# A gated state-space and MLP kernel: the first 512 tokens laid out four to a partition

## The chip, the cores and the metric

The kernel runs on one core of a Trainium2 chip. The time is the device time of one execution in microseconds, as the median of several runs. A profile of one execution stands beside it; its span leaves out what lies around the instructions.

## The reference

The input is x, 2048 tokens of 448 features in bf16. Two branches are computed and mixed by a gate of each token:

```python
g = sigmoid((x * gate_w).sum(-1, keepdims=True))
# branch A: a diagonal state-space layer
dt = exp(log_dt); Lam_bar = exp(dt * Lam)                # Lam = Lambda_re + i Lambda_im, 448 states
B_bar = ((Lam_bar - 1) / Lam)[:, None] * (B_re + i B_im)
Bu = einsum("bld,pd->blp", x, B_bar)
h[t] = Lam_bar * h[t-1] + Bu[t]                          # over the 2048 tokens
a = 2 * einsum("blp,dp->bld", h, C_re + i C_im).real + x * Dskip
# branch B: an MLP
b = silu(x @ w1) @ w2                                    # 448 -> 1792 -> 448
out = g * a + (1 - g) * b
```

## The kernel before

The tokens are cut into four stretches of 512 (`CH`), each of four blocks of 128. All of it is written as a list of operations with reads, writes, an estimated cost and a priority. A planner (`Plan.order`) lays them in order: TensorE's operations stay in the written order, those of the other engines are taken as they come ready by the estimates. It also gives each PSUM result its bank or pair of banks. `Waits` then puts semaphores between the engines, and the order is fixed before the kernel runs.

For a stretch `tc`:

- *Load* (lines 401 and 402 for the first stretch, `load_xn` for the others): x arrives in `xnat` as [128 partitions, block, 448]. The token of partition p and block b is 128 b + p. The first stretch comes in two transfers of two blocks each, `xn00` on SP's queue and `xn01` on ScalarE's, each the first of its queue; the first columns of w1 follow behind them in the same two queues.
- *Turning* (`x0_transposes` for the first stretch, line 478; `x_transposes`, line 508): TensorE transposes the blocks, VectorE and ScalarE copy the results into `xT` (lines 486 and 488; 516 and 518), features on partitions and the stretch's 512 tokens side by side, block after block.
- *Products* (`x_products`, line 663): two tiles at a time share a pair of PSUM banks. An "F" tile is 128 of the 1792 columns of x @ w1; ScalarE evicts it with SiLU into `aT`. A "B" tile is one of the seven slots of real and imaginary parts of U, the input of the states. `evict` copies U out of PSUM: for the first stretch VectorE (line 640, three evictions of two tiles and one of one tile), for the others ScalarE (line 642).
- *Lanes* (`lanes`): VectorE rotates U by tables of sines and cosines, runs the recurrence as a scan along the 512 columns (line 736), and rotates back into `H[tc]`, seven slots of 512 columns. The scan needs the columns in time order.
- *MLP output* (`ffn2`, line 774): for each block, 14 matmuls with the block's 128 columns of `aT` as weights; ScalarE scales by 1 - g, and a DMA adds the result to `Tb` (which is `xnat`'s space and already holds g x Dskip).
- *Readout* (`readout`, line 795): for each block, seven matmuls with 128 columns of `H[tc]` as weights and the output weights `CP` as the moving side; VectorE multiplies by g and adds `Tb` (line 798) into one of five buffers `ot`, and SP stores the 128 rows (line 801).

The gate (`gates`) works on `xnat` rows, each partition by itself. TensorE's written order is: products of the first stretch (eight F tiles, the seven B tiles, six F tiles) and, with the second stretch's turning in between, the second stretch's B tiles; then the readout weights and the MLP output of the first stretch; the F tiles of the second stretch, and so on. The first stretch's readout stands behind the second stretch's MLP output.

Of the kernel before, what the change touches and what calls it, by code (L numbers as in the profile page):

```python
# [17 lines left out]
CH = 512  # L18
# [3 lines left out]
NSLOT = 7  # L22
NOT = 5
# [253 lines left out]
def bass_gated_mix__ssm_conv_s5__dense_activation_silu__prompt_kernel(nc, A_x, A_Lambda_re, A_Lambda_im, A_B_re, A_B_im, A_C_re, A_C_im,  # L277
               A_log_dt, A_Dskip, B_x, B_w1, B_w2, gate_w, out):
    with ExitStack() as ctx:
        E = ctx.enter_context  # L280
        P = Plan()

        def sb(name, shape, dtype):
            return E(nc.sbuf_tensor(name, list(shape), dtype))

        x2, out2 = A_x[0], out[0]

        xnat = sb("xnat", [128, NTB, D_MOD], BF16)
# [4 lines left out]
        CP = sb("CP", [128, NSLOT, D_MOD], BF16)  # L293
# [6 lines left out]
        H = [H2C[:, 0:3584].rearrange("p (s n) -> p s n", s=NSLOT) if k == 2 else sb(f"H{k}", [128, NSLOT, CH], BF16) for k in range(4)]  # L300
# [11 lines left out]
        ot = [sb(f"ot{k}", [128, D_MOD], BF16) for k in range(NOT)]  # L312
# [41 lines left out]
        def sem():  # L354
            _s[0] += 1
            return E(nc.semaphore(name=f"d{_s[0]}"))

        def bk(t, k=0):
            return ps[:, t.bank + k, :]

        def bk2(t):
            return ps[:, t.bank:t.bank + 2, :]
# [4 lines left out]
        def act_cost(n, aps=0):  # L367
            return 0.17 + n * 0.000833 + 0.09 * aps
# [4 lines left out]
        def ACT(fn, r, w, cost, prio, tag=""):  # L373
            return P.add("act", fn, r, w, cost, prio, tag=tag)

        def DVE(fn, r, w, cost, prio, tag=""):
            return P.add("dve", fn, r, w, cost, prio, tag=tag)
# [4 lines left out]
        def PE(fn, r, w, cost, tag=""):  # L382
            return P.add("pe", fn, r, w, cost, 0, tag=tag)
# [3 lines left out]
        def load(q, dst, src, name, nbytes, prio=None, after=()):  # L387
            nl[0] += 1
            prio = nl[0] if prio is None else prio
            P.add(q, lambda e: e.dma_start(dst, src), list(after), name.split(), 0.6 if q == "pool" else 0.5, prio, sem(), nbytes, tag="ld " + name)  # L390
# [3 lines left out]
        def load_w1(q, k, a, b):  # L394

            cols = slice(w1cuts[k], w1cuts[k + 1])
            src = B_w1[320:448, cols] if a == 3 else B_w1[128 * a:128 * b, cols].rearrange("(b p) f -> p b f", p=128)
            load(q, w1s[:, 3, cols] if a == 3 else w1s[:, a:b, cols], src, " ".join(f"w1_{k}_{i}" for i in range(a, b)),
                 256 * (b - a) * (cols.stop - cols.start))

        for h, q in enumerate(("sp", "act")):
            load(q, xnat[:, 2 * h:2 * h + 2, :], x2[256 * h:256 * h + 256, :].rearrange("(b p) d -> p b d", p=128), f"xn0{h}", 256 * 896)
        load_w1("sp", 0, 0, 2)
        load_w1("act", 0, 2, 3)
        load_w1("act", 0, 3, 4)
# [217 lines left out]
        def evict(pair, tk):  # L623

            kinds = [t[0] for t in pair]
            for k, n in ((0, 2),) if pair[0][:2] == pair[-1][:2] and len(pair) == 2 else ((0, 1), (1, 1))[:len(pair)]:
                kind, tc, a = pair[k]
                step = pair[k + 1][2] - a if n == 2 else 1
                sl = slice(a, a + step * (n - 1) + 1, step)
                names = [t[2] for t in pair[k:k + n]]  # L630
                src = (lambda: bk2(tk)) if n == 2 else (lambda k=k: bk(tk, k)[:, None, :])
                if kind == "F":
                    dst = aT[tc % 2][:, sl, :]
                    ACT(lambda e, src=src, dst=dst: e.activation(dst, src(), AF.Silu),  # L634
                        [tk, "tbl"], [f"aT{tc % 2}_{m}" for m in names], act_cost(512 * n), 2.5, "silu")
                    continue
                U, un = UG[tc % 2], f"U{tc % 2}_"
                dst = U[:, sl, :]
                if tc == 0:
                    DVE(lambda e, src=src, dst=dst: e.tensor_copy(dst, src()), [tk], [f"{un}{m}" for m in names], 0.15 + 0.53 * n, 2.6, "U")  # L640
                else:
                    ACT(lambda e, src=src, dst=dst: e.activation(dst, src(), AF.Copy), [tk], [f"{un}{m}" for m in names], act_cost(512 * n), 5, "U")  # L642
                if 3 in names:
                    load("pool", U[0:64, 7, :], U[64:128, 3, :], un + "7a", 65536, 9, [un + "3"])
                    load("pool", U[64:128, 7, :], U[0:64, 3, :], un + "7b", 65536, 9, [un + "3"])

        def x_products(tiles, fill={}, wait=()):
# [22 lines left out]
            def half(k, h):  # L670
                if h == 0 and pairs[k][0] == ("F", 0, 0):
                    def zero(pe):
                        for n in range(NFILL):
                            for b, p in enumerate((slice(64, 128), slice(0, 64))):
                                r = pe.matmul(bk(toks[k], b)[:, 0:128], ones[p, 0:128], ones[p, 0:128], start=True, stop=True)  # L675
                        return r
                    PE(zero, [], [toks[k]], NFILL * 0.11, "fill")
                    steps(k, 0, 0, 2)
                    steps(k, 0, 2, 4)
                else:  # L680
                    steps(k, h, 0, len(part[h])).own = h == 1
                if h:
                    evict(pairs[k], toks[k])
# [102 lines left out]
        def readout(tb):  # L786
            tc, o = tb // 4, (tb % 4) * 128
            t0 = tb * 128
            cuts = [(0, D_MOD)] if tb + 1 < NTB else [(0, 192), (192, 320), (320, D_MOD)]
            for n, (a, b) in enumerate(cuts):  # L790
                tk = Ps()

                def mm(pe, tk=tk, a=a, b=b):
                    for s in range(NSLOT):
                        r = pe.matmul(bk(tk)[:, 0:b - a], H[tc][:, s, o:o + 128], CP[:, s, a:b], start=(s == 0), stop=(s == NSLOT - 1))  # L795
                    return r
                PE(mm, [f"H{tc}_{s}" for s in range(7)] + [f"CP{s}" for s in range(NSLOT)], [tk], NSLOT * (0.0025 + (b - a) / 2400), f"C{tc}")
                DVE(lambda e, tk=tk, a=a, b=b: e.scalar_tensor_tensor(ot[tb % NOT][:, a:b], bk(tk)[:, 0:b - a], g[:, tb:tb + 1],  # L798
                                                                      Tb[:, tb, a:b], ALU.mult, ALU.add),
                    [tk, f"g_{tc}", f"Tb{tb}"], [f"ot{tb % NOT}{n}"] if len(cuts) > 1 else [f"ot{tb % NOT}{m}" for m in range(3)], 0.2 + (b - a) / 960, 3, "out")  # L800
                P.add("sp", lambda e, a=a, b=b: e.dma_start(out2[t0:t0 + 128, a:b], ot[tb % NOT][:, a:b]),
                      [f"ot{tb % NOT}{n}"], [], 0.3, 1, outs[tb % NOT], 128 * 2 * (b - a), tag="st")

        def readout_weights(k):
# [56 lines left out]
        def C(*tbs):  # L861
            return [lambda tb=tb: readout(tb) for tb in tbs]
# [56 lines left out]
```

## Time and profile before

| what | value |
|---|---|
| median of the runs | 141.48 us (141.35, 141.48, 143.88) |
| profiled execution | 141.25 us, span 139.5 us |
| TensorE busy | 135.9 us, 97% of the span |
| VectorE busy | 122.0 us, 87% |
| ScalarE busy | 90.3 us, 65% |
| issue of the first x loads to landing | 2.9 us (SP), 3.2 us (ScalarE), 224 KB each |
| granted TensorE clock | 0.998 of full speed |

In the profile's rows, PE is TensorE's matmuls, PEld its weight loads, DVE is VectorE, ACT ScalarE, POOL GpSimd, SP the engine that issues most transfers. A group's row has the line of the code, the engine, the operation, out<-in with shapes, the count, then busy time and mean ns of one, then the idle time of the engine before them and what ended it. A timeline row begins with start and duration in us from the span's start. Matmuls are pipelined: one of 512 columns is drawn with about 0.38 us, but they follow each other faster.

### The profile page before, as it was taken

Reading aid. Unit: us, or ns where it says so; the run is one execution under the profiler, and the core shown is the slowest. Engines: PE = TensorE matmul, PEld = TensorE weight load, DVE = VectorE, ACT = ScalarE, POOL = GpSimd, SP = SyncE. Lnnn points to the kernel's source line nnn. Section 1 sums busy time; section 2 is a strip of 40 time slices with the busy share of each in tenths; the row PEclk is TensorE's granted clock in tenths of the full one; section 3 lists DMA queues with packets and bytes.
Section 4 is the critical chain, followed back from the end, with each engine's and each line's share of the span. In section 5 each row is a group of like instructions: output and inputs, shape, how many; then the busy total and the mean of one; then the engine's idle time right before and its main releaser. Section 6 shows DMA issues by size and latency. Waiting matters only on the chain.

```text
span 139.5 us, 3000 instructions
## 1 busy us (share of the span) xinstructions
PE 135.9 (97%) x1201; PEld 67.0 (48%) x1201; DVE 122.0 (87%) x179; ACT 90.3 (65%) x157; POOL 39.2 (28%) x72
## 2 busy tenths in 40 slices
PE   7999999999999999999999999999999999999992
PEld 2445454455544544455544544444455555555561
DVE  0319999999999999999999999999999999997053
ACT  3349768999989999823694887799931268312300
POOL 7134040100248440227733001824000314022220
PEclk9999999999999999999999999999999999999999
DMA  4998999510156770104976200674202322323242
GB/s 136 337 294 243 363 320 238 177 42 0 31 79 94 129 110 1 38 15 73 157 131 155 38 5 0 95 133 79 38 4 97 66 33 36 83 83 61 40 94 71
DMA packets 17956, 14.71 MB, mean 105 GB/s; under 512 B 2835, under 2 KB 17814, under 8 KB 17942
## 3 DMA queue, kind: packets, MB, share of 16 engines
q0 software_dynamic: 6064, 5.51, 24.8%
q1 hardware_dynamic: 11318, 8.65, 20.7%
q10 hardware_dynamic: 560, 0.36, 0.8%
q8 instruction: 9, 0.15, 0.4%
q14 instruction: 5, 0.04, 0.1%
HBM read 7.17 MB, written 1.84 MB: 65 GB/s over the span
## 4 chain that ended last, share of the span: by engine, by line
PE 97%; DVE 0%; issue 0%
PE ps L663 46%; PE ps L774 31%; PE ps L795 15%; PE ps L463 2%; PE ps L508 1%; PE ps L478 1%; PE ps L814 1%; PE ps L604 1%; DVE ot L798 0%; PE ps L675 0%; PE ps L464 0%; PE ps L536 0%
## 5 line engine op out<-in xcount | busy, mean ns | idle before, releaser
L663 PE MATMUL ps<-xT,w1s 64*128 64x512 bf16 x392 | 48.5, 378 | 0.0
L774 PE MATMUL ps<-w2s,aT 128*128 128x448 bf16 x224 | 43.2, 353 | 0.0
L634 ACT ACTIVATE aT<-ps 128x1024 bf16<-128x1024 f32 (+1 forms) x30 | 28.7, 969 | 8.5 <-PE ps L663 8.4
L774 PEld LDWEIGHTS ps<-w2s,aT 128*128 128x128 bf16 x224 | 21.7, 98 | 20.4 <-ACT xnat L849 0.4
L663 PEld LDWEIGHTS ps<-xT,w1s 64*128 64x128 bf16 x392 | 19.7, 94 | 22.3 <-DVE xT L486 0.7
L663 PE MATMUL ps<-xT,BT 64*128 64x512 bf16 x196 | 25.8, 376 | 0.0
L782 POOL DMA_DIRECT2D xnat<-fe x16 | 14.1, 900 | 37.9 <-ACT fe L780 37.2
L780 ACT ACTIVATE fe<-ps,g 128x448 bf16<-128x448 f32 x16 | 10.1, 632 | 21.1 <-PE ps L774 21.0
L390 POOL DMA_DIRECT2D UG<-Gf x27 | 14.7, 549 | 20.9 <-DVE Gf L736 20.4
L736 DVE TENSOR_TENSOR_SCAN Gf<-rc,gin,H 128x512 f32<-128x512 f32 x14 | 17.2, 1268 | 0.0
L795 PE MATMUL ps<-CP,H 128*128 128x448 bf16 (+2 forms) x98 | 16.4, 326 | 0.0
L663 PEld LDWEIGHTS ps<-xT,BT 64*128 64x128 bf16 x196 | 10.8, 94 | 11.1 <-DVE Gf L562 0.2
L798 DVE SCALAR_TENSOR_TENSOR ot<-ps,g,xnat 128x448 bf16<-128x448 f32 (+2 forms) x18 | 10.8, 622 | 6.0 <-issue 4.6
L390 POOL DMA_DIRECT2D UG<-UG x8 | 4.8, 597 | 29.2 <-ACT UG L642 17.4
L704 DVE TENSOR_TENSOR H<-UG,COS 128x3584 bf16<-128x3584 bf16 (+4 forms) x10 | 12.6, 1266 | 0.0
L795 PEld LDWEIGHTS ps<-CP,H 128*128 128x128 bf16 x98 | 8.9, 98 | 7.5 <-DVE k L752 0.4
L642 ACT ACTIVATE UG<-ps 128x1024 bf16<-128x1024 f32 (+1 forms) x12 | 10.7, 923 | 1.4 <-PE ps L663 1.4
L842 ACT ACTIVATE junk<-xg 128x448 bf16<-128x448 bf16 x16 | 9.2, 574 | 2.1 <-DVE xg L704 2.0
L849 ACT ACTIVATE xnat<-xnat,g 128x448 bf16<-128x448 bf16 x16 | 9.8, 671 | 0.2
L704 DVE TENSOR_TENSOR PI<-UG,SIN 128x512 bf16<-128x512 bf16 (+2 forms) x13 | 9.1, 722 | 0.0
L704 DVE TENSOR_TENSOR PO<-UG,SIN 128x1536 bf16<-128x1536 bf16 (+1 forms) x8 | 8.7, 1087 | 0.1
L736 DVE TENSOR_TENSOR_SCAN Gf<-rc,gin,H2C 128x512 f32<-128x512 f32 x7 | 8.5, 1265 | 0.0
(102 smaller groups left out, 126.5 us busy)
## 6 DMA issues: line engine op xcount, KB each, us to landing
UG<-Gf POOLq DMA_DIRECT2D x21, 128.0 KB, 2.5
xnat<-fe POOLq DMA_DIRECT2D x16, 112.0 KB, 2.6
out_dram<-ot SPq DMA_DIRECT2D x15, 112.0 KB, 1.7
w2s<-in_B_w_dram SPq DMA_DIRECT2D x1, 1568.0 KB, 11.8
xnat<-in_A_x_dram SPq DMA_DIRECT2D x3, 448.0 KB, 6.1
w1s<-in_B_w_dram SPq DMA_DIRECT2D x1, 576.0 KB, 6.2
UG<-UG POOLq DMA_DIRECT2D x8, 64.0 KB, 2.2
H2C<-in_A_C_re_dram SPq DMA_DIRECT2D x2, 196.0 KB
```

Of the source, the lines that this page charges most:

```text
L390: P.add(q, lambda e: e.dma_start(dst, src), list(after), name.split(), 0.6 if q == "pool" else 0.5, prio, sem(), nbytes, tag="ld " + name)
L634: ACT(lambda e, src=src, dst=dst: e.activation(dst, src(), AF.Silu), [tk, "tbl"], [f"aT{tc % 2}_{m}" for m in names], act_cost(512 * n), 2 ...
L642: ACT(lambda e, src=src, dst=dst: e.activation(dst, src(), AF.Copy), [tk], [f"{un}{m}" for m in names], act_cost(512 * n), 5, "U")
L663: r = pe.matmul(bk(toks[k], b), weights(tile, p0, p0 + 64, i), xT[p0:p0 + 64, i, tc * CH:(tc + 1) * CH], start=(h == 0 and n == 0), stop=( ...
L704: DVE(lambda e: e.tensor_tensor(o, a, b, op), r, w, dve_cost(n, 2), prio, tag)
L736: DVE(lambda e, s=s, b=b, init=init: e.tensor_tensor_scan(Gf[:, s, :], rc[:, b:b + 1].to_broadcast([128, CH]), A[:, s, :], init, ALU.mult, ...
L774: r = pe.matmul(bk(tk)[:, 0:D_MOD], aT[tc % 2][:, fb, o:o + 128], w2s[:, fb, :], start=(fb == 0), stop=(fb == NFB - 1))
L780: ACT(lambda e: e.activation(f[:, :], bk(tk)[:, 0:D_MOD], AF.Copy, scale=g1[:, tb:tb + 1]), [tk, f"g1_{tc}"], [fn], act_cost(448, 1), 7, "fe")
L782: P.add("pool", lambda e: e.dma_start(Tb[:, tb, :], f[:, :], accum_op=ALU.add), [fn, f"Tb{tb}"], [f"Tb{tb}"], 0.94, 2, sem(), 115000, tag= ...
L795: r = pe.matmul(bk(tk)[:, 0:b - a], H[tc][:, s, o:o + 128], CP[:, s, a:b], start=(s == 0), stop=(s == NSLOT - 1))
L798: DVE(lambda e, tk=tk, a=a, b=b: e.scalar_tensor_tensor(ot[tb % NOT][:, a:b], bk(tk)[:, 0:b - a], g[:, tb:tb + 1], Tb[:, tb, a:b], ALU.mul ...
L849: ACT(lambda e, tb=tb: e.activation(Tb[:, tb, :], xnat[:, tb, :], AF.Copy, scale=g[:, tb:tb + 1]), [f"xd{tc}", f"g_{tc}"], [f"Tb{tb}"], ac ...
```

## The change

Only the first stretch is touched, in four places.

- *Load:* partition p takes the four neighbouring tokens 4p to 4p + 3; block b holds token 4p + b. The two transfers still bring two blocks each, so a partition's part of one transfer is two neighbouring rows of x, 1792 bytes in one piece.
- *Eviction of U* (line 640): `xT`, and with it the product in PSUM, now has its columns in the order (block, partition). The VectorE copy reads it in that order and writes column (b, t) to place 4 t + b, so U is in time order again.
- *Readout* (line 796 after): the weights of block tb are the columns tb, tb + 4, tb + 8, ... of `H[0]`.
- *Store* (lines 802 and 803 after): block tb's 128 rows go to the rows 4p + tb of the output.

What works token by token (F tiles, gate, `ffn2`, `Tb`) stays as it is, in the new order of tokens.

```diff
-            load(q, xnat[:, 2 * h:2 * h + 2, :], x2[256 * h:256 * h + 256, :].rearrange("(b p) d -> p b d", p=128), f"xn0{h}", 256 * 896)
+            load(q, xnat[:, 2 * h:2 * h + 2, :], x2[0:CH, :].rearrange("(p b) d -> p b d", b=4)[:, 2 * h:2 * h + 2, :], f"xn0{h}", 256 * 896)
...
                 if tc == 0:
-                    DVE(lambda e, src=src, dst=dst: e.tensor_copy(dst, src()), [tk], [f"{un}{m}" for m in names], 0.15 + 0.53 * n, 2.6, "U")
+                    DVE(lambda e, src=src, dst=dst: e.tensor_copy(dst.rearrange("p s (t b) -> p s b t", b=4), src().rearrange("p s (b t) -> p s b t", b=4)), [tk], [f"{un}{m}" for m in names], 0.15 + 0.53 * n, 2.6, "U")
...
-                        r = pe.matmul(bk(tk)[:, 0:b - a], H[tc][:, s, o:o + 128], CP[:, s, a:b], start=(s == 0), stop=(s == NSLOT - 1))
+                        h = H[tc][:, s, o:o + 128] if tc else H[0][:, s, tb:CH:4]
+                        r = pe.matmul(bk(tk)[:, 0:b - a], h, CP[:, s, a:b], start=(s == 0), stop=(s == NSLOT - 1))
...
-                P.add("sp", lambda e, a=a, b=b: e.dma_start(out2[t0:t0 + 128, a:b], ot[tb % NOT][:, a:b]),
+                rows = out2[t0:t0 + 128] if tc else out2[0:CH].rearrange("(p b) d -> p b d", b=4)[:, tb, :]
+                P.add("sp", lambda e, a=a, b=b, rows=rows: e.dma_start(rows[:, a:b], ot[tb % NOT][:, a:b]),
                       [f"ot{tb % NOT}{n}"], [], 0.3, 1, outs[tb % NOT], 128 * 2 * (b - a), tag="st")
```

## The prediction

> **What bounds the kernel now.** I read the busy table and the slices first, then the chain that ended last, then the groups of the touched lines by form, then the timeline and the waits of the two stretches that the change touches: the start, and the end of the first stretch's products.
>
> ```profile
> span 139.5 us, 3000 instructions
> PE 135.9 (97%) x1201; PEld 67.0 (48%) x1201; DVE 122.0 (87%) x179; ACT 90.3 (65%) x157; POOL 39.2 (28%) x72
> PE   7999999999999999999999999999999999999992
> DVE  0319999999999999999999999999999999997053
> DMA  4998999510156770104976200674202322323242
> PE 97%; DVE 0%; issue 0%
> ```
>
> TensorE is busy in every slice but the first and the last, and the chain is TensorE from 0.76 us to the last eviction. So the time moves only if TensorE starts its real work at another time, works longer, or stops in the middle. VectorE is full from slice 3 on and has room only in the last five slices. The DMA row is full from slice 1 to 6: the opening loads go as fast as the queues move bytes.
>
> The groups of the touched instructions (count | busy us, mean ns | idle before):
>
> ```profile
> L795 PE MATMUL ps<-CP,H 128*128 128x448 bf16 x28 | 5.5, 352 | 0.0
> L795 PEld LDWEIGHTS ps<-CP,H 128*128 128x128 bf16 x28 | 2.7, 98 | 2.6
> L640 DVE CAST UG<-ps 128x1024 bf16<-128x1024 f32 x3 | 3.6, 1216 | 0.0
> L640 DVE CAST UG<-ps 128x512 bf16<-128x512 f32 x1 | 0.7, 682 | 0.0
> L516 DVE COPY xT<-ps 128x1024 bf16<-128x1024 bf16 x1 | 0.7, 679 | 0.0
> ```
>
> The first two are the first stretch's readout (67.5 to 73.2 us), the others the first stretch's evictions and the copy of the next stretch's turned tokens. And the stretch where these evictions stand against TensorE (start us, us, ...):
>
> ```profile
> 18.43 1.22 DVE L640 CAST UG<-ps 128x1024 bf16<-128x1024 f32 x1
> 19.57 0.42 DVE L524 TENSOR_SCALAR Gf<-Gf 128x512 f32<-128x512 f32 x1
> 19.90 0.68 DVE L640 CAST UG<-ps 128x512 bf16<-128x512 f32 x1
> 20.50 0.68 DVE L516 COPY xT<-ps 128x1024 bf16<-128x1024 bf16 x1
> ...
> 19.94 0.38 PE L663 MATMUL ps<-xT,w1s 64*128 64x512 bf16 x2
> ...
> 21.45 0.38 PE L663 MATMUL ps<-xT,BT 64*128 64x512 bf16 x1
> ```
>
> And who waits there (engine line <- releaser: us, times, longest), in the waits of 18 to 22 us:
>
> ```profile
> PEld ps L663 <- DVE xT L516: 0.2, 1, 0.2
> ```
>
> The third eviction ends at 19.65, and the TensorE pair that takes over its two banks in the plan (F0, tiles 11 and 12) starts at 19.94. The copy of xT ends at 21.18, and the first pair that reads it starts at 21.45, its weight load having waited 0.2 us for just that copy. From VectorE's end to TensorE's start 0.2 to 0.3 us pass anyway, so there is next to no slack at either place.
>
> **The change part by part.** No instruction is added, removed or reordered on any engine: the planner's costs are the same, and the orders of the two programs differ in access patterns alone. So each edit is priced by the new duration of the old instruction.
>
> *First load.* Two transfers (SP and ACT queues, first of each) bring 224 KB each. Before, a partition gets two pieces of 896 B from rows 128 apart, 512 pieces in all; now two neighbouring rows, one piece of 1792 B, 256 in all. The trace's packet records give 41 ns for 896 B, 27 ns for 512 B and 65 ns for 1536 B, a line of 37 ns per KB and some 8 ns per piece. No packet of 1792 B was moved; by that line it takes 75 ns. On the 16 DMA engines: 512 x 41 / 16 = 1.31 us before, 256 x 75 / 16 = 1.19 after, 0.12 saved. Bounds: nothing, if a piece costs exactly twice (82 ns); 0.3, if the dozen long first pieces (300 to 570 ns, some 0.3 us per engine in all) are halved too. I take 0.12, which rests on three rows of a line.
>
> Who waits for it: the transposes start at 3.62, just after the two halves land at 3.58 and 3.93; the warm-up matmuls end at 3.5 to 3.7, so here alone hardly 0.1 can be won. But the weights of w1 follow in the same queues and TensorE waits for them twice more (at 6.24, when the second block has landed at 6.14, and at 7.73, when the third has at 7.63), all behind the same bytes. They come 0.12 earlier, and so does all TensorE work behind them; the parameters' chain on VectorE starts from a TensorE step (8.76) and moves along. Sum: -0.12.
>
> *Eviction (L640).* Same 1024 or 512 elements, read in the same order, each written 8 bytes from the last instead of 2. The f32 source already holds it to one element at a time: 1.216 - 0.682 = 0.534 us for 512 elements, 1.04 ns each, where the bf16 copy L516 does 1024 in 0.679. No row of the trace writes single elements with gaps; L486, L516 and L612 write runs of 64. Bounds: nothing, if a write of 2 bytes takes its step wherever it goes; and, for a second step per element, again 1.04 ns each, 1.07 us per 1024. Less than nothing I exclude: the elements stay as many, and their pace is already one at a time. Let x be what 1024 elements cost more. VectorE works through its list without a gap, so the third eviction ends 3x late and the xT copy 3.5x late, TensorE's pair at 21.45 starts 3.5x late, and as TensorE has no gap afterwards, all of it reaches the end. What queues behind on VectorE (phase tables, xg, lanes) is late by the same and hides behind nothing, but it needn't: TensorE is late as well. I take x = 0, since one element at a time is already the slow pace; both ends are kept: 0 to 3.5 x 1.07 = 3.74 us.
>
> On this the pages of the Trainium skill disagree. "Vector Engine (DVE) Microarchitecture Reference", section 5.2, says that a port keeps its rate only while neighbouring elements come in pairs of adjacent words, and gives 1.71 ns instead of 1.05 for a destination that hops at each element (measured there with 4-byte words and far hops). By it x is an estimated 0.68, the sum +2.3 us. "SBUF — State Buffer", section "Door 1: The DMA port swizzle", says that lines are 16 bytes and that two hits on a line are enough, so that bf16 may be strided up to 8 elements for free; four elements give two hits, x = 0. No run here shows either so far; the first is a rival below.
>
> *Readout weights.* 28 weight loads of 128 columns, each column 8 bytes from the next. They take 98 ns beside matmuls that follow each other every 5.30 us / 28 = 189 ns, so 91 ns of cover each. Loads of 64 and of 128 rows take 93 to 98, and no row has gaps between columns. Bounds: 0, and at four times the time (392 ns) 28 x (392 - 189) = 5.7 us. Twice the time (196) would cost 0.2. I take 0: nothing shows up until a load has nearly doubled.
>
> *Stores.* The four stores of the first stretch still move 128 pieces of 896 B each, now with gaps in memory. They land in 1.7 us, five output buffers rotate, and nothing but SP's next store stands behind them. 0; were each 1 us longer, the next use of a buffer (five blocks on) would still be far off.
>
> *Sum.* The profiled execution took 141.25 us (139.5 span and 1.75 around it): 141.25 - 0.12 + 0 + 0 + 0 = 141.13. The median of the runs is 0.23 above that execution, so I forecast **141.36**.
>
> **Rivals.**
> 1. *Scattered writes cost part of a step.* For it: each element goes to 8 bytes of its own, where now four share them. Against it: the 1.04 ns per element is already the pace of one at a time. At half a step more, x = 0.53, +1.87 us: 143.2 on the median's scale; between 141.7 and 144.2 for x from 0.1 to 0.85. The rule of the first page named above falls in here, at an estimated 143.7.
> 2. *They cost a whole step or more.* Place: L640, through the banks and the xT copy; price 3.74 us, 145.1 (+2.6%). It decides from x = 0.85 on, where 2% is passed. For it: VectorE has no gap before 128 us and TensorE none after 21. Against it: nothing in the trace that moves 2-byte elements shows such a pace.
> 3. *The weight load leaves its cover.* At 250 ns, 28 x 61 = 1.7 us: 143.1; 2% is passed at about 300 ns. For: no row has gaps. Against: it must grow by more than 91 ns.
> 4. *The edit of the load does nothing, the rest neither:* pieces of twice the size at twice the time, 141.5. For: the DMA row is full, which speaks for bytes and not for pieces as the limit.
>
> **How the numbers follow.** Forecast 0.58 (141.0 to 141.4), rival 4 0.10 (141.4 to 141.6), rival 1 0.19, rival 2 0.08, rival 3 0.04, and 0.01 that the start wins much more. The forecast and rival 4 together fill 141.0 to 141.6; reaching into rival 1 to 144.0 and to 140.9 below leaves some 0.15 out. Two per cent, about what a measurement of this kernel can tell from no change, is 2.8 us: slower than 144.3 is rival 2 and the upper part of rival 3, 0.10; faster 0.01; within 0.89.
>
> **What would show it.** Right: L640 still at 1.216 and 0.682 us, its third start near 18.3; the xn00 and xn01 loads landing about 0.1 earlier, and the weight load for the second F pair near 6.1 instead of 6.24; readout weight loads under 189 ns and its 28 matmuls in 5.3 us. Wrong: L640 above 1.3 us together with TensorE waiting for L640 or L516 around 20 to 22 us; weight loads of the readout near 200 ns or more; or an unchanged landing of the first loads.

## The result and the profile after

The changed kernel is slower: 146.38 us median of six runs (144.82 to 146.56) beside 141.41 before, ratio 1.0326 with the 95% interval 1.0268 to 1.0384. Its profiled execution took 146.56 us with a span of 144.7. A few executions (143.88 us of the kernel before, 147.87 of e1 below) are over 1.5% longer than the others of their kernel; they stand in the medians and ranges given here, but not in the ratios. The page of the changed kernel, the rows that answer to those shown of before:

```profile
span 144.7 us, 3000 instructions
PE 138.3 (96%) x1201; PEld 68.2 (47%) x1201; DVE 126.0 (87%) x179; ACT 90.4 (62%) x157; POOL 38.7 (27%) x72
PE   7999964999999999999999999999999999999992
DVE  0329999998999999999999999999899999999043
PEclk9999997799999999999999999999999999999999
```

TensorE has a hole in slices 5 and 6, counted from 0 (18 to 25 us), and just behind it the clock row falls to 7 for two slices. VectorE has 4.0 us more work. Where that sits (groups of VectorE, 14 to 26 us: count | busy us, mean ns | idle before):

```profile
L640 DVE CAST UG<-ps 128x1024 bf16<-128x1024 f32 x3 | 7.3, 2424 | 0.0
L640 DVE CAST UG<-ps 128x512 bf16<-128x512 f32 x1 | 1.3, 1280 | 0.0
```

1216 ns became 2424, and 682 became 1280: x, what 1024 elements cost more, is 1.21 us. The chain that ended last, 15 to 26 us (start us, us, what), and the waits of TensorE:

```profile
15.66 2.35 DVE UG L640
18.02 0.52 DVE Gf L527
18.53 2.34 DVE UG L640
20.87 0.25 DVE Gf L562
21.12 2.35 DVE UG L640
23.48 0.05 issue
23.52 2.54 PE ps L663 x11
```

```profile
PEld ps L663 <- DVE UG L640: 2.0, 1, 2.0
PE ps L663 <- DVE UG L640: 1.9, 1, 1.9
PE ps L508 <- DVE UG L640: 1.0, 1, 1.0
```

From 15.66 us on, the end is set by VectorE. TensorE stops twice: ahead of the second stretch's transposes, whose banks the second eviction holds (1.0 us), and ahead of the F pair whose banks the third one holds (1.9 us). That pair starts at 23.52 where it started at 19.94 before, 3.58 us later.

Then the clock. These are stretches of 3.41 us around the hole (us, length, PE busy (x), PEld, DVE, ACT, POOL, PEclk, DMA, GB/s):

```profile
20.35:23.76 3.41, 0.88 (x36) 0.68 (x38) 3.41 (x5) 2.12 (x3) 1.34 (x2) 1.00 1.03 232
23.76:27.17 3.41, 3.41 (x20) 1.24 (x18) 3.41 (x9) 0.63 (x1) 0.00 (x0) 0.50 0.61 201
27.17:30.60 3.43, 3.43 (x34) 1.55 (x32) 3.43 (x12) 3.43 (x7) 0.00 (x0) 1.00 0.00 0
```

In the first TensorE was busy for 0.88 us of 3.41; through the whole of the second it ran at half speed, and exactly from its end at full speed again. The runs fall into two groups by that: 144.82 and 145.10 us at a granted clock of 1.0, and 146.36 to 146.56 at 0.988. So some 3.5 us are the wait, and some 1.5 the half-speed stretch, which four of the six runs had.

### The profile page after: what moved, and what is told of

Read it like the earlier page. It is cut to its first block, busy times and chain, and to the rows that moved or that the text cites. A ratio compares the mean times of both kernels' runs of the same rounds, so it can differ in the third digit from the quotient of the medians.

```text
span 144.7 us, 3000 instructions
## 1 busy us (share of the span) xinstructions
PE 138.3 (96%) x1201; PEld 68.2 (47%) x1201; DVE 126.0 (87%) x179; ACT 90.4 (62%) x157; POOL 38.7 (27%) x72
## 3 DMA queue, kind: packets, MB, share of 16 engines
HBM read 7.17 MB, written 1.84 MB: 62 GB/s over the span
## 4 chain that ended last, share of the span: by engine, by line
PE 89%; DVE 9%; issue 0%
PE ps L663 40%; PE ps L774 29%; PE ps L796 15%; DVE UG L640 5%; PE ps L463 2%; DVE BT L612 1%; DVE Gf L555 1%; DVE Gf L527 1%; PE ps L816 1%; PE ps L478 1%; PE ps L508 1%; DVE Gf L524 0%; DVE Gf L562 0%; DVE ot L799 0%; PE ps L675 0%; PE ps L604 0%
## 5 line engine op out<-in xcount | busy, mean ns | idle before, releaser
L663 PE MATMUL ps<-xT,w1s 64*128 64x512 bf16 x392 | 50.5, 391 | 1.9 <-DVE UG L640 1.9
L663 PEld LDWEIGHTS ps<-xT,w1s 64*128 64x128 bf16 x392 | 20.5, 97 | 25.4 <-issue 2.7
L782 POOL DMA_DIRECT2D xnat<-fe x16 | 14.6, 935 | 39.0 <-ACT fe L780 37.7
L390 POOL DMA_DIRECT2D UG<-Gf x27 | 15.5, 624 | 19.8 <-DVE Gf L736 19.6
L640 DVE CAST UG<-ps 128x1024 bf16<-128x1024 f32 (+1 forms) x4 | 8.6, 2138 | 0.0
```

The lines of the kernel that those rows point to most:

```text
L640: DVE(lambda e, src=src, dst=dst: e.tensor_copy(dst.rearrange("p s (t b) -> p s b t", b=4), src().rearrange("p s (b t) -> p s b t", b=4)), ...
L663: r = pe.matmul(bk(toks[k], b), weights(tile, p0, p0 + 64, i), xT[p0:p0 + 64, i, tc * CH:(tc + 1) * CH], start=(h == 0 and n == 0), stop=( ...
L782: P.add("pool", lambda e: e.dma_start(Tb[:, tb, :], f[:, :], accum_op=ALU.add), [fn, f"Tb{tb}"], [f"Tb{tb}"], 0.94, 2, sem(), 115000, tag= ...
```

## The experiments

Theory 1 was that the scattered writes alone make the evictions long, and that TensorE pays for VectorE's lateness, whatever its cause. Theory 2 was that the layout as a whole (load, weights, stores) carries a part.

**e1: the scattered eviction alone, on the kernel before.**

```diff
-e.tensor_copy(dst, src())
+e.tensor_copy(dst.rearrange("p s (t b) -> p s b t", b=4), src().rearrange("p s (b t) -> p s b t", b=4))
```

> The kernel before with the scattered eviction of U alone; the load, the readout weights and the stores stay as before, so the first stretch's scan runs over columns in another order. Theory 1 (the writes alone, 2 bytes every 8, cost a second step per element): L640 at 2.42 and 1.28 us as in the changed kernel, and the whole loss is there, 144.8 to 146.6 us. Theory 2 (the loss comes from the layout as a whole: load, weights or stores carry a part): L640 slow but the time at least 1 us below the changed kernel's.

146.01 us (144.9 to 147.87), ratio 1.0291, interval 1.023 to 1.0353. Its groups:

```profile
L640 DVE CAST UG<-ps 128x1024 bf16<-128x1024 f32 x3 | 7.3, 2427 | 0.0
```

The same long evictions and the same loss, without the rest of the change. Its profiled execution (145.33 us, span 143.5) shows no half-speed stretch behind the wait, so the span has the wait without it: 143.5 - 139.5 = 4.0 us. Of these, 0.36 us were there before any eviction: TensorE's parameter step (L536) starts at 9.12 us instead of 8.76.

**e2: all of the change but the scattered eviction.** In line 640 the copy is as before.

> The changed kernel with the eviction as it was, so the first stretch's scan runs over columns in the order in which they were loaded. Theory 1: L640 back at 1.22 and 0.68 us and the time at that of before, 141.1 to 141.5, since the load's 0.1 to 0.2 us is at most what is left; readout weight loads 98 ns. Theory 2: 142 us or more.

141.61 us beside 141.73 of the kernel before, ratio 0.9986, interval 0.9968 to 1.0004. The evictions take 1211 ns again, and theory 2 is out: load, readout weights and stores cost nothing that can be measured. The readout's weight loads, with their columns 8 bytes apart, did get longer, and it doesn't show (weight loads of 64 to 82 us):

```profile
L796 PEld LDWEIGHTS ps<-CP,H 128*128 128x128 bf16 x28 | 3.2, 114 | 2.1
```

114 ns instead of 98, under a matmul every 189.

**e3: the same lateness with plain writes.** On the kernel before, each eviction of the first stretch is done twice.

```diff
-e.tensor_copy(dst, src())
+(e.tensor_copy(PI[:, sl, :], src()), e.tensor_copy(dst, src()))[1]
```

> The kernel before with each eviction of U for the first stretch done twice, first into PI (not yet in use then), then into U; all writes side by side. VectorE is as long away as with the scattered writes (2 x 1.14 us), without any of them. Theory 1 (TensorE pays for VectorE's lateness through the banks and the xT copy, whatever makes it late): 144.5 to 146.5 us, with TensorE idle ahead of its steps near 21 and 23 us, and in some runs a granted clock near 0.99, in others 1.0. A rival, in which scattered writes also slow TensorE or the lanes by themselves: below 144.

146.47 us (145.96 to 147.47), ratio 1.0348, interval 1.0311 to 1.0384: the changed kernel's time. Its waits and clock:

```profile
PE ps L663 <- DVE UG L640: 1.9, 1, 1.9
PE ps L508 <- DVE UG L640: 1.0, 1, 1.0
```

```profile
PEclk9999997799999999999999999999999999999999
```

The same two stops and the same half-speed stretch (23.60 to 27.01 us by the clock's records), with no write that leaves a gap. The granted clock was 0.988 in three runs and 0.975 in the fourth, where I had expected some at 1.0. So the loss needs nothing of the scattered writes but their time.

**e4: the gaps on the read side.** The changed kernel, with U written side by side.

```diff
-dst.rearrange("p s (t b) -> p s b t", b=4), src().rearrange("p s (b t) -> p s b t", b=4)
+dst.rearrange("p s (t b) -> p s t b", b=4), src().rearrange("p s (b t) -> p s t b", b=4)
```

> The changed kernel with the eviction of U written side by side and read from PSUM with a step of 128 columns (512 bytes), the same U. Theory 1a (what costs is a write of 2 bytes in 8 bytes of its own): L640 at 1.22 and 0.68, time 141.1 to 141.5. Theory 1b (any access with gaps costs a second step, on the read side too): L640 near 2.4, time 144.8 to 146.6.

141.64 us, ratio 1.0001, interval 0.9991 to 1.0011.

```profile
L640 DVE CAST UG<-ps 128x1024 bf16<-128x1024 f32 x3 | 3.6, 1208 | 0.0
```

The same reordering of the same data costs nothing when PSUM is read with a step of 512 bytes and SBUF is written in a row. The loss is one choice: which side of this copy carries the gaps.

**m1: the forms by themselves.**

> None of the reference's work: a row of copies of 1024 elements, first on VectorE and at the same time on ScalarE, each form twice: from f32 PSUM to bf16 side by side, at every 2nd, 4th and 8th element, in the changed kernel's order on the write side and on the read side, in runs of 2 and of 4 elements with gaps as long; then bf16 SBUF to SBUF plain, with the write at every 4th, with the read at every 4th. After that 16 matmuls each with weight columns at a step of 1, 4, 8 and 32 elements, and with the moving side read in time order, at every 4th and at every 8th element. Theory 1a (a 2-byte write that has 8 bytes to itself costs a second step): plain 1.22, every 4th 2.4, every 8th 2.4 or more, runs of 4 elements (8 bytes) 1.22; every 2nd, two to 8 bytes, 1.2. A rival, theory 1c (any 2-byte write whose neighbour isn't next costs it): every 2nd and runs of 2 also 2.4 and 1.8. ScalarE: if it has the same limit, 1.03 goes to about 2; if not, it stays. Weight loads with gaps: 98 ns by theory 1, since the changed kernel's took that.

One execution. VectorE, second round (the first differs by at most 0.09 us), 1024 elements from f32 PSUM to bf16 in SBUF. In order: plain; written at every 2nd, 4th, 8th element; the changed kernel's order on the write side; on the read side; runs of 2; runs of 4 (timeline: start us, us):

```profile
36.22 1.23 DVE L311 CAST Y<-ps 128x1024 bf16<-128x1024 f32 x1
37.48 1.30 DVE L311 CAST Y<-ps 128x1024 bf16<-128x1024 f32 x1
38.81 2.46 DVE L311 CAST Y<-ps 128x1024 bf16<-128x1024 f32 x1
41.31 4.78 DVE L311 CAST Y<-ps 128x1024 bf16<-128x1024 f32 x1
46.13 2.47 DVE L311 CAST Y<-ps 128x1024 bf16<-128x1024 f32 x1
48.63 1.22 DVE L311 CAST Y<-ps 128x1024 bf16<-128x1024 f32 x1
49.89 1.22 DVE L311 CAST Y<-ps 128x1024 bf16<-128x1024 f32 x1
51.15 1.22 DVE L311 CAST Y<-ps 128x1024 bf16<-128x1024 f32 x1
```

From this source, the time for single elements goes with the bytes stepped over: 4 bytes 1.30, 8 bytes 2.46, 16 bytes 4.78, some 3.5 bytes per ns once that is slower than the 1.04 ns of an element. Runs of 2 and of 4 elements with gaps as long are free; on average they step over 4 bytes per element, which single elements take nearly for free too, so whether runs help across wider gaps is not shown. The form that the changed kernel uses has 2.47, as there. Theory 1c is out, and 1a has the place right but not the size: the cost grows with the distance and is no fixed second step. ScalarE shows the same (plain, every 2nd, every 4th):

```profile
27.43 1.02 ACT L310 ACTIVATE Z<-ps 128x1024 bf16<-128x1024 f32 x1
28.49 1.34 ACT L310 ACTIVATE Z<-ps 128x1024 bf16<-128x1024 f32 x1
29.86 2.51 ACT L310 ACTIVATE Z<-ps 128x1024 bf16<-128x1024 f32 x1
```

so by these figures the same writes would take as long on ScalarE; no run moved the eviction there. TensorE, by the starts of its matmuls of 512 columns: 216 ns apart with weight columns at steps of 1, 4, 8 and 32 elements (the loads with gaps 112 to 148 ns, not the 98 that I expected); but with the moving side at every 4th element 451, at every 8th 900, and in time order (a step of 256 bytes) 865. The clock isn't the reason: it was 1.0 up to 27.50 us, 0.5 up to 41.15, 1.0 up to 47.98 and 0.5 from there, and the 865, the 451 and the 900 ns stand unchanged on both sides of these three places.

**e5: the reordering on TensorE's moving side.** The changed kernel, U evicted as before.

```diff
-xT[p0:p0 + 64, i, tc * CH:(tc + 1) * CH]
+xT[p0:p0 + 64, i, 0:CH].rearrange("p (b t) -> p t b", b=4)    # first stretch's B products
```

> The changed kernel with U evicted as before, and the change of order put into the first stretch's B products: their moving side reads xT with a step of 128 columns (256 bytes), so that PSUM already holds time order. If TensorE reads with gaps at full pace: 141.1 to 141.6, as the kernel before. If the moving side takes a second step for each column as VectorE's writes do: 28 matmuls in 14 pairs, each pair 0.216 more, 3 us, so 144 to 145, and 64x512 rows of xT,BT near 0.6 us for the first stretch.

160.38 us, ratio 1.1308, interval 1.1258 to 1.1357, far beyond both expectations. Its matmuls of 11 to 38 us, and the clock row of its page:

```profile
L666 PE MATMUL ps<-xT,BT 64*128 64x512 bf16 x49 | 24.7, 1038 | 0.0
```

```profile
PEclk9999555555999999999999999999999999999999
```

A column costs four times its step here, not twice, as m1 has it: the pairs of these matmuls start 0.86 us apart, before and after 16.17 us, where the clock goes to half until 40.06 although TensorE is drawn as busy all the way. There are 49 of them, in some 25 pairs, and not the 28 in 14 that I had counted: 25 x (0.86 - 0.216) is 16 of the 18.6 us. One piece of its chain, 41 matmuls of this stretch, takes 17.70 us.

**e6: the measured cost in the plan.** The changed kernel with `0.12 + 1.15 * n` for the eviction in the planner.

> The changed kernel, with the planner told the eviction's measured cost (0.12 + 1.15 per tile instead of 0.15 + 0.53), so that it lines VectorE's work up anew: the four evictions and the xT copy follow each other, and the phase tables come after. TensorE is then held up by less: the three table steps of about 1.2 us in all no longer stand between the evictions, so by theory 1 142.9 to 144.0 without a half-speed stretch of the clock. If TensorE pays for the evictions' own length only at the banks: no gain, 144.8 or more.

144.93 us (144.75 to 145.80), ratio 1.0237, interval 1.0192 to 1.0282. The range that I gave to theory 1 was missed; the time lies in that of "no gain". The three long evictions follow each other and TensorE's stops shrink to 0.5 and 1.5 us, but the phase tables now come late, and ScalarE with them. From its chain:

```profile
15.82 6.92 DVE UG L640 x3
...
24.52 1.02 ACT aT L634
25.54 0.52 ACT SIN L560
26.06 0.61 ACT COS L563
...
30.42 1.41 ACT UG L642 x2
```

Three of its four runs have the clock at 1.0 and take 144.75 to 145.02, no less than the changed kernel's 144.82 and 145.10 at that clock. One run in four has the half-speed stretch, too few to call it rarer. The lateness itself is not gone: in this chain it goes round by ScalarE.

**e7 and e8: two tokens per partition.** Each of the two loads takes 256 neighbouring tokens, two per partition; the pieces are still 1792 bytes. e7 writes U at every 2nd element, e8 reads it with the gaps.

```diff
-x2[0:CH, :].rearrange("(p b) d -> p b d", b=4)[:, 2 * h:2 * h + 2, :]
+x2[256 * h:256 * h + 256, :].rearrange("(p b) d -> p b d", b=2)
...
-h = H[0][:, s, tb:CH:4]
+h = H[0][:, s, 256 * (tb // 2) + tb % 2:256 * (tb // 2) + 256:2]
...
+dst.rearrange("p s (h t b) -> p s h b t", h=2, b=2), src().rearrange("p s (h b t) -> p s h b t", h=2, b=2)    # e7
+dst.rearrange("p s (h t b) -> p s h t b", h=2, b=2), src().rearrange("p s (h b t) -> p s h t b", h=2, b=2)    # e8
```

> The changed kernel with two neighbouring tokens per partition in each of the two loads instead of four over both: the load's pieces are still 1792 bytes, U is written at every 2nd element (4 bytes) instead of every 4th, the readout's weights lie two columns apart, the stores' rows two apart. If a write costs by the bytes that it steps over, as the row of copies had it (plain 1.22, every 2nd 1.30 to 1.35, every 4th 2.46, every 8th 4.8): L640 at 1.30 and 0.72, x = 0.1, TensorE later by at most 0.35 us, so 141.6 to 142.1 beside 141.7 before. If in this kernel any gap on the write side costs a second step: L640 near 2.4 and 144.8 to 146.6.

> The same layout with two tokens per partition, U written side by side and read from PSUM with a step of 128 columns. L640 at 1.21 and 0.68; what is left of the change is the load in half as many pieces. If the 0.1 to 0.2 us by which the third block of w1 lands earlier reach the end: 141.5 beside 141.7, ratio 0.999. If they are lost at the start (TensorE's half-speed opening and the order of the waits there): ratio 1.000.

e7: 141.45 us beside 141.61 of the kernel before, just below the range that I gave, ratio 0.999, interval 0.9973 to 1.0006; e8: 141.50, ratio 0.9995, interval 0.9974 to 1.0015. e7's evictions:

```profile
L640 DVE CAST UG<-ps 128x1024 bf16<-128x1024 f32 x3 | 3.9, 1303 | 0.0
```

A step of 4 bytes instead of 8 takes the loss away, inside the kernel as in the row of copies. What is left of the change, the load above all, cannot be told from the kernel before by e2, e4, e7 or e8, and none of them beats it beyond its interval.

## Why the prediction was wrong

**The eviction: the step that failed.** I took x = 0 because VectorE already went one element at a time. That the source sets the pace is right only as long as the destination keeps up, and x is 1.21 us. The upper bound was a little low too: "a second step per element", 1.07 us, was a guess at the form of the cost, and m1 shows a cost by bytes stepped over. No row of the trace had a single-element write with gaps, so the trace alone could not price it. The runs of 64 in L486, L516 and L612 were no evidence: in m1 runs of 2 are already free.

Of the two rules weighed, that of the Trainium skill's "SBUF — State Buffer" (two hits on a 16-byte line are enough, bf16 free up to a step of 8) would make x zero, and the runs contradict it: a step of 4 elements takes 2.46 us and one of 8 takes 4.78. The Trainium skill's "Vector Engine (DVE) Microarchitecture Reference", section 5.2, had the direction right. The estimate of x = 0.68 came from its row for hops of 4 KiB and is too small for this form; the same table has 2.50 to 2.51 ns for a destination that steps 24 words at each element, which would have made an estimated 1.5, so the measured 1.21 lies between its rows.

**The path: right, the size a little over.** That there is little slack at the banks and at the xT copy, and that VectorE's lateness goes through to the end, is what e3 shows with plain writes. The formula gives 3.5 x 1.21 = 4.2 us; the spans at a clock of 1.0 (143.0, 143.3 and e1's 143.5, beside 139.5) give 3.5 to 4.0. Two things were too simple. VectorE in the changed kernel:

```profile
21.04 2.42 DVE L640 CAST UG<-ps 128x1024 bf16<-128x1024 f32 x1
23.26 0.46 DVE L524 TENSOR_SCALAR Gf<-Gf 128x512 f32<-128x512 f32 x1
23.63 1.28 DVE L640 CAST UG<-ps 128x512 bf16<-128x512 f32 x1
24.71 0.72 DVE L516 COPY xT<-ps 128x1024 bf16<-128x1024 bf16 x1
```

An instruction starts before the one ahead is drawn as ended, so what counts is from start to start: 2.22 us from the third eviction to the next instruction, beside 1.14 before. That is 1.08 more, and 3.5 x 1.08 = 3.8 us. And the 0.2 to 0.3 us from VectorE's end to TensorE's start, which I took for a fixed delay, was mostly slack: the third eviction now ends at 23.46 and TensorE's pair starts at 23.52. Of the 3.58 us by which this pair is later, 0.33 are the opening's (L536 at 9.09 us instead of 8.76). In e1 the pair that reads the xT copy starts at 25.52 instead of 21.45, 4.07 us later, of which 0.36 are the opening's: 3.7 us are left for the evictions.

**What the sum had no term for: the clock.** Rival 2 named the place and priced it at 145.1, and the runs at full clock lie there, 144.82 and 145.10; that it fits so well is partly luck, since its x was too small and its 3.5 x too large. The other four runs have 1.5 us more. In their profile a stop of some 3 us leaves a stretch of 3.41 us with little work, and the next one runs at half speed: at most 3.41 / 2 = 1.7 us. The Trainium skill's "TensorE: Matmul & The Clock Gate", section "What's actually happening", tells of a free-running window of 3413 ns, an idle one bringing the clock to half; the trace agrees with the length and adds that 0.88 us of work in the window was not enough. The other profiles fit a window that runs by itself, if it is counted on in steps of 3.41 us from where the clock first rose: in e3, which lost the clock, the window ahead has 0.76 us of work; in e1 and e6, which kept it, the same kind of stop falls across two windows, and the emptier one still has 1.56 and 1.84. By this, whether a run pays the 1.5 us hangs on where its windows lie, which no run here sets. The kernel before has a granted clock of 0.988 too, in 3 of the 53 runs that list it, but the changed kernel in 4 of 6. I had read the mean clock of before (0.998) and stopped there.

**The load: priced right by the piece, too small to see.** The new pieces take 74 ns (75 forecast; the line in the prediction, worked out again, gives 73), and the third block of w1 landed at 7.38 us instead of 7.63. But the first half of x landed no earlier, at 3.61 us instead of 3.58, where I had put 0.1 less. In the profiles of the kernels, m1 aside, TensorE reached full clock anywhere from 3.5 to 6.7 us after the start, the changed kernel's latest of all (6.69, before 5.77), and its opening was 0.33 us later, not earlier. A gain of 0.12 us is 0.0008 of the time and inside every interval of e2, e4 and e8.

**Weights and stores: right.** Loads of 114 ns under 189, nothing lost in e2. That the stores cost nothing is shown only together with the rest, by e2. Rivals 3 and 4: the first didn't happen, the second describes e2 as well as the forecast does. Two slips in the prediction change nothing: VectorE's row has room in the last four slices, not five, and rival 1 at x = 0.85 comes to 144.3, not 144.2.

## What to carry to other kernels

When a copy reorders data, ask which side carries the gaps: here f32 PSUM was read with steps of 512 and 1024 bytes for nothing, while single bf16 elements written 8 bytes apart doubled the copy. Before an off-path engine is called cheap, find the instruction whose banks or outputs the busy engine takes next and measure the gap: with 0.3 us of it, all but some 0.2 us of VectorE's lateness became the kernel's. And price a stop of the busy engine with the clock in it: here a stop of some 3 us cost 1.5 us more in four runs of six.

## What the runs showed of the hardware that I had not expected

- From f32 in PSUM, writes of single 2-byte elements to SBUF cost by the distance stepped over, on VectorE and ScalarE alike: 1.30 and 1.34 us for 1024 at 4 bytes, 2.46 and 2.51 at 8. Runs of two elements with gaps as long are free (1.22).
- From bf16 in SBUF, VectorE wrote every 4th element in 1.32 to 1.34 us, about half of the 2.46 that the f32 source in PSUM needs for the same places; ScalarE took 2.51 to 2.54 from there, no less than from PSUM. So the 3.5 bytes per ns are not a figure of the destination alone, and why is open.
- TensorE's moving side is the sensitive one: 216 ns per 512 columns in a row, 451 at a step of 8 bytes, 900 at 16 and 865 at 256; its weight loads take 112 to 148 ns at steps of 4 to 32 elements, and the matmuls still follow each other at 216.
- While such matmuls ran, the granted clock fell to half with TensorE drawn as busy throughout: in e5 from 16.17 to 40.06 us, in m1 from 27.50 and again from 47.98. It did not change their own pace, but the plain matmuls among them in e5 started 427 ns apart.
